# First loads in 256 KB pieces ordered by need, with a flight limit, and larger weight sums, in a two-layer convolution and joint kernel

## The chip, the cores and the metric

The kernel runs on one core of one Trainium2 chip. The time is the device time of one execution in microseconds (us), as a median of several executions. Engines are named as the profile names them: PE is TensorE's matmuls, PEld its weight loads, DVE is VectorE, ACT is ScalarE, POOL is GpSimd, SP is SyncE, which issues all loads here. All times inside an execution count from the start of its profiled span.

Ratios are the mean time of one kernel's fast runs over that of the other's fast runs of the same rounds, so they are not quite the ratios of the medians quoted beside them. The "granted clock" of a table is the share of PE's full clock that the chip allowed (1.00 is all of it).

## The reference, cut to what matters

```python
B, T, D, K, U = 2, 4000, 512, 5, 8            # x: [B,T,D], w1, w2: [K,D,D], all bf16
h = sum of 5 taps: xp[:, i:i+T, :] @ w1[i]    # then gelu, then every second row
f = sum of 5 taps: hp[:, i:i+T1, :] @ w2[i]   # then gelu, then every second row
fe = f @ w_f ; ge = g @ w_g
j = tanh(fe[:, :, None, :] + ge[:, None, :, :])
return j @ w_o                                 # [2, 1000, 8, 512]
```

Because only every second row of h is kept, the kernel works on four phases of the time axis (row number modulo 4). A fast-convolution scheme replaces part of the products: some operands are differences or sums of phases (named a0, a1, a2, a3, b1, b3), and some weights are sums of taps: 2·(tap 1 + tap 3), and (tap 0 + tap 4) minus or plus tap 2.

## The kernel before: the parts that matter

The first 1000 rows of layer 1 are split into two tiles, here "tile 1" (254 columns) and "tile 2" (246 columns); a larger "tile 3" follows. Tile 1's input comes by plain loads and is transposed on PE; all other inputs come by transposing DMA. In tile 1, output blocks m = 0 and 1 are computed directly from five taps, while blocks 2 and 3 use the operands and weight sums.

```python
for rt in range(2): load_xr(rt)                   # 2 x 512 KB of x
for i in (0, 1, 3, 4, 2): load_w1("sp", i)        # 5 taps x 512 KB
for ph in (2, 3, 1, 0): load_x(0, ph, 272, 528)   # tile 2, transposing DMA, then later tiles
...
warm_mm(12)                                       # matmuls on zeros while the loads travel
for pp in range(2):                               # pp 0: even phases, pp 1: odd phases
    for rt in range(2): ...                       # 8 PE transposes; pp 0 copied by DVE, pp 1 by ACT
...
for w in ("a0", "a1", "a2", "b3"): t0.xf(w)       # DVE operands of tile 1
for w in ("b1", "a3"): t0.shift(w); t0.xf(w)      # an ACT copy, then DVE
wsum13(...)                                       # DVE: add, then times 2
wsum04(..., 2); wsum04(..., 3)                    # DVE: 3 ops of 128x512 each
for i in (0, 1, 3): direct(i)                     # PE
filt("a0", "b1"); direct(4); filt("b3", "a3"); direct(2); filt("b2", "a1", "a2")
for w in ("a0", "b1", "a3"): t1.shift(w)          # tile 2, ACT
for w in ("a0", "b1", "b3", "a1"): t1.xf(w)       # tile 2, DVE
wsum04(..., 0); t1.xf("a2"); t1.xf("a3"); wsum04(..., 1)
... t0.gelu(0), t0.gelu(1), t0.post(2), t0.post(3)   # first evictions of tile 1 on DVE
```

Each engine runs its instructions in the order in which the program lists them. An instruction that waits holds up everything behind it on its engine: in the changed kernel below, DVE stands idle for 2.31 us until 11.66 us, although all inputs of a sum that is listed later had landed by 8.20 us.

## Time and profile before

| | |
|---|---|
| time, median of the 3 runs known at first | 281.95 us (281.63 to 282.59); with a fourth run 281.79 |
| PE busy, of a span of 280.3 us | 273.9 us |
| first weight matmul on PE | 8.99 us |
| DVE's first eviction of tile 1 starts | 26.12 us |
| chain of waits stays on PE from | 42.15 us |

The head of the page (span, then busy time of each engine, its share and its number of instructions), kernel before:

```profile
span 280.3 us, 3870 instructions
PE 273.9 (98%) x1436; PEld 137.8 (49%) x1436; DVE 188.0 (67%) x250; ACT 160.3 (57%) x191; POOL 30.2 (11%) x39
```

Averaged over the span, PE is the limit. The start is different. Next is the table by stage of the kernel before: per stretch its length, then the busy time of each engine, the granted clock, and the DMA share and rate. (The DMA share adds up packet times, and it can exceed 1.)

```profile
core 0: us, PE busy (x) PEld busy (x) DVE busy (x) ACT busy (x) POOL busy (x), PEclk, DMA share, GB/s
6.00:16.00 10.00, 8.95 (x98) 8.07 (x97) 8.68 (x13) 3.93 (x4) 0.18 (x3) 1.00 1.25 266
16.00:26.00 10.00, 10.00 (x96) 9.06 (x94) 9.42 (x16) 4.70 (x7) 0.12 (x1) 1.00 0.96 208
```

From 6 to 26 us DVE is busy for 18.1 of 20 us. It is nearly as full as PE (18.95 us). The list of waits of PE from 2 to 46 us (who waited for whom, total us, times, longest) shows how little PE waits:

```profile
PE acc L298 <- DMA w_sb<-in_w_dram: 1.1, 1, 1.1
PE acc L298 <- DVE xt_55 L287: 0.7, 2, 0.5
PE acc L298 <- DVE xs_50 L287: 0.2, 1, 0.2
```

The timeline of DVE (start, busy us, engine and line, operation, names, shapes, count) just before its first eviction, which is the last line (the first line is the sum of taps 1 and 3):

```profile
12.13 1.22 DVE L287 TENSOR_TENSOR w_t<-w_sb 128x2048 bf16<-128x2048 bf16 x1
13.38 0.69 DVE L423 TENSOR_SCALAR w_t<-w_t 128x2048 bf16<-128x2048 bf16 x1
...
21.10 0.68 DVE L287 TENSOR_TENSOR ssum_70<-w_sb 128x512 f32<-128x512 bf16 x1
21.82 1.29 DVE L287 TENSOR_TENSOR w_t<-ssum_70,w_sb 128x512 bf16<-128x512 f32 x2
23.03 0.67 DVE L287 TENSOR_TENSOR xs_49<-xs_49 128x984 bf16<-128x984 bf16 x1
23.61 0.67 DVE L287 TENSOR_TENSOR xt_54<-xt_54,xs_49 128x984 bf16<-128x984 bf16 x1
24.19 0.68 DVE L287 TENSOR_TENSOR ssum_71<-w_sb 128x512 f32<-128x512 bf16 x1
24.91 1.29 DVE L287 TENSOR_TENSOR w_t<-ssum_71,w_sb 128x512 bf16<-128x512 f32 x2
26.12 0.75 DVE L499 SCALAR_TENSOR_TENSOR ty_67<-acc,cs_65 128x254 f32<-128x254 f32 x2
```

From 21.10 us on, these lines follow one another with no idle time: weight sum of block 0, tile 2's operands a2 and a3, weight sum of block 1, first eviction. The chain of work that ended last (start, us, what) shows where DVE stops mattering:

```profile
40.89 1.12 DVE xt_55 L287
42.02 0.14 issue
42.15 234.13 PE acc L298 x1112
```

After 42.15 us PE runs almost to the end. So the time is what happens before that moment, plus a rest of about 240 us.

### The profile page before, as it was taken

To read this page: it belongs to the slowest core of one execution; us is meant where nothing else is said; L and a number is where in the kernel's file an instruction comes from. 1 tells how busy PE (TensorE), PEld (TensorE's weight loads), DVE (VectorE), ACT (ScalarE), POOL (GpSimd) and SP (SyncE) were. 2 spreads that over 40 slices of the span, in tenths; PEclk is the share of its full clock that TensorE was granted. 3 is DMA by queue.
4 is the path that set the end of the run, shared out by engine and by line. 5 is a ranking of instruction groups with operands and counts; after the bars stand their busy time and mean duration, and the time that the engine had idled before them with its cause. 6 is when DMAs were issued, how large, how long until landed. Compare 5 with 4: busy or idle time off the path is not lost.

```text
span 280.3 us, 3870 instructions
## 1 busy us (share of the span) xinstructions
PE 273.9 (98%) x1436; PEld 137.8 (49%) x1436; DVE 188.0 (67%) x250; ACT 160.3 (57%) x191; POOL 30.2 (11%) x39
## 2 busy tenths in 40 slices
PE   8899989999999999999999999999999999999995
PEld 3799934444444444444444444444444444444442
DVE  0989797956896766686424363676776775666764
ACT  2533949328426533932336565948957957966930
POOL 1000000099992000000000000000000000000000
PEclk9999999999999999999999999999999999999999
DMA  7999999990000000000000020444454445444444
GB/s 251 291 179 201 213 211 191 316 325 3 4 0 0 2 0 0 0 2 0 0 0 4 0 75 5 155 155 154 135 169 151 150 144 170 145 155 145 155 150 140
DMA packets 54719, 31.85 MB, mean 114 GB/s; under 512 B 31646, under 2 KB 54446, under 8 KB 54702
## 3 DMA queue, kind: packets, MB, share of 16 engines
q1 hardware_dynamic: 54702, 31.62, 41.8%
q8 instruction: 11, 0.18, 0.3%
q14 instruction: 6, 0.05, 0.1%
HBM read 7.86 MB, written 16.38 MB: 87 GB/s over the span
## 4 chain that ended last, share of the span: by engine, by line
PE 84%; SPq 6%; DVE 5%; issue 2%; ACT 1%; DMA 1%; DVEq 0%
PE acc L298 84%; SPq L330 4%; SPq L316 2%; DMA xs_49<-in_x_dram 1%; ACT xt_55 L291 1%; DVE xs_50 L287 1%; DVE xt_55 L287 1%; DVE w_t L287 1%; DVE ty_68 L499 1%; DVE ty_68 L287 0%; DVE xt_54 L287 0%; SPq L321 0%; DVE ty_67 L499 0%; DVE ty_69 L499 0%; DVE ssum_71 L287 0%
## 5 line engine op out<-in xcount | busy, mean ns | idle before, releaser
L298 PE MATMUL acc<-wo_sb,jT 128*128 128x512 bf16 (+1 forms) x504 | 108.3, 378 | 0.0
L298 PEld LDWEIGHTS acc<-wo_sb,jT 128*128 128x128 bf16 x504 | 49.3, 98 | 58.8
L298 PE MATMUL acc<-xt_55,w_sb 128*128 128x500 bf16 (+1 forms) x192 | 42.1, 357 | 0.2 <-DVE xt_55 L287 0.2
L291 ACT ACTIVATE jT<-feT_80,geT 128x1000 bf16<-128x1000 f32 (+6 forms) x44 | 35.8, 889 | 0.0
L291 ACT ACTIVATE jT<-feT_79,geT 128x1000 bf16<-128x1000 f32 (+4 forms) x40 | 35.1, 948 | 0.0
L298 PE MATMUL acc<-xt_54,w_sb 128*128 128x500 bf16 (+1 forms) x160 | 33.2, 342 | 0.0
L298 PEld LDWEIGHTS acc<-xt_55,w_sb 128*128 128x128 bf16 x192 | 18.6, 98 | 18.7 <-issue 0.9
L291 ACT ACTIVATE cs_65<-acc 128x500 f32<-128x500 f32 (+2 forms) x13 | 7.0, 538 | 27.3 <-PE acc L298 27.3
L298 PEld LDWEIGHTS acc<-xt_54,w_sb 128*128 128x128 bf16 x160 | 15.6, 98 | 13.0
L291 ACT ACTIVATE cs_66<-acc 128x500 f32<-128x500 f32 (+2 forms) x13 | 7.0, 536 | 21.8 <-PE acc L298 21.7
L298 PE MATMUL acc<-xs_49,w_sb 128*128 128x254 bf16 (+2 forms) x112 | 15.6, 286 | 1.1 <-DMA w_sb<-in_w_dram 1.1
L291 ACT ACTIVATE ost_93<-acc 128x512 bf16<-128x512 f32 x10 | 6.0, 597 | 16.4 <-PE acc L298 16.4
L679 DVE CAST ost_82<-acc 128x512 bf16<-128x512 f32 x11 | 7.6, 691 | 10.3 <-PE acc L298 10.3
L679 DVE CAST ost_88<-acc 128x512 bf16<-128x512 f32 x10 | 6.9, 692 | 10.3 <-PE acc L298 10.3
L298 PE MATMUL acc<-xs_49,w_t 128*128 128x246 bf16 (+2 forms) x72 | 13.8, 315 | 0.0
L287 DVE TENSOR_TENSOR ty_68<-ty_68,acc 128x1000 f32<-128x1000 f32 (+2 forms) x9 | 9.7, 1079 | 5.7 <-PE acc L298 5.7
L287 DVE TENSOR_TENSOR ty_67<-ty_67,acc 128x1000 f32<-128x1000 f32 (+2 forms) x9 | 9.7, 1078 | 5.1 <-PE acc L298 5.1
L298 PEld LDWEIGHTS acc<-xs_49,w_sb 128*128 128x128 bf16 x112 | 10.8, 97 | 4.0 <-DMA w_sb<-in_w_dram 1.2
L291 ACT ACTIVATE ost_87<-acc 128x512 bf16<-128x512 f32 x10 | 5.9, 593 | 11.4 <-PE acc L298 11.4
L287 DVE TENSOR_TENSOR ty_69<-ty_69,acc 128x1000 f32<-128x1000 f32 (+1 forms) x8 | 8.5, 1061 | 4.2 <-PE acc L298 4.1
L298 PE MATMUL acc<-xt_55,w_t 128*128 128x500 bf16 (+1 forms) x48 | 10.0, 341 | 0.5 <-DVE xt_55 L287 0.5
L679 DVE CAST ost_86<-acc 128x512 bf16<-128x512 f32 (+1 forms) x12 | 7.7, 646 | 2.6 <-PE acc L298 2.6
(116 smaller groups left out, 363.2 us busy)
## 6 DMA issues: line engine op xcount, KB each, us to landing
w_sb<-in_w_dram SPq DMA_DIRECT2D x10, 512.0 KB, 7.9
out_dram<-ost_82 SPq DMA_DIRECT2D x11, 128.0 KB, 1.9
out_dram<-ost_84 SPq DMA_DIRECT2D x10, 128.0 KB, 1.9
out_dram<-ost_86 SPq DMA_DIRECT2D x10, 128.0 KB, 1.9
out_dram<-ost_90 SPq DMA_DIRECT2D x10, 128.0 KB, 1.9
out_dram<-ost_83 SPq DMA_DIRECT2D x9, 128.0 KB
out_dram<-ost_85 SPq DMA_DIRECT2D x9, 128.0 KB
out_dram<-ost_87 SPq DMA_DIRECT2D x9, 128.0 KB
```

Of the source, the lines that this page charges most:

```text
L287: pl.op(eng, lambda e: e.tensor_tensor(out=o.ap, in0=a.ap, in1=b.ap, op=op), (a, b), (o,))
L291: pl.op("act", lambda e: e.activation(o.ap, i.ap, func, scale=scale, bias=0.0 if bias is None else bias.ap), rd, (o,))
L298: ins = e.matmul(o.ap, lhsT=l.ap, rhs=r.ap, start=start and n == 0, stop=stop and n == len(pairs) - 1, skip_group_check=not check)
L316: return pl.dma(eng, lambda e: e.dma_start(dst.ap, src), (), (dst,))
L330: pl.dma("sp", lambda e: e.dma_start_transpose(out=dst.ap, in_=src), (), (dst,))
L499: pl.op("dve", lambda e, o=o, f=f: e.scalar_tensor_tensor(out=o.ap, in0=d.ap, scalar=f, in1=c.ap, op0=ALU.mult, op1=add), (d, c), (o,))
L679: pl.op("dve", lambda e, o=o, v=v: e.tensor_copy(out=o.ap, in_=v.ap), (v,), (o,))
```

## The change

The intent is to start PE earlier. The first loads become pieces of 256 KB, in the order in which PE needs them, with at most four under way. PE then turns the even phases alone, starts with taps 0, 2 and 4 (which need only even phases), and turns the odd phases in between. The larger weight sums are meant to relieve DVE. The diff, cut:

```diff
-    NWARM = 12
+    NWARM = 7
+    FLIGHT = 4
...
+        def load_lead(dst, src):       # waits for the load issued FLIGHT places earlier
...
-            load_xr(rt)
-        for i in (0, 1, 3, 4, 2):
-            load_w1("sp", i)
+            load_xr(0, rt)                       # even phases, 256 KB each
+        for i in (0, 2, 4):
+            load_w1(i, 0)                        # output columns 0..255 of a tap
+        for rt in range(2):
+            load_xr(1, rt)                       # odd phases
+        for i, h in ((1, 0), (3, 0), (0, 1), (1, 1), (3, 1), (4, 1), (2, 1)):
+            load_w1(i, h)
...
-                if pp:
+                if rt:                           # of each pair of copies, one on DVE, one on ACT
                     act(o, pv, ACT.Copy)
...
+        turn(0)
+        warm_mm(3)
...
+            if eng == "dve":
+                act(v, v, ACT.Copy, scale=2.0)   # the doubling goes to ACT
-        def wsum04(wsb, wt, eng, m):
+        def wsum04(wsb, wt, eng, m, nm=1):       # nm blocks in one op
...
+        t0.shift("a0")
+        for w in ("a1", "a2", "a0"):
             t0.xf(w)
+        for i in (0, 2):
+            direct(i)
+        turn(1)
         for w in ("b1", "a3"):
             t0.shift(w)
+        for w in ("b3", "b1", "a3"):
             t0.xf(w)
+        for i in (4, 1, 3):
+            direct(i)
         wsum13(w1_sb, w1_t, "dve")
-        wsum04(w1_sb, w1_t, "dve", 2)
-        wsum04(w1_sb, w1_t, "dve", 3)
+        wsum04(w1_sb, w1_t, "dve", 2, 2)
+        filt("a0", "b1", "b3", "a3", "b2", "a1", "a2")
...                                               # both t0.gelu calls now come before t1.shift
-        for w in ("a0", "b1", "b3", "a1"):
+        for w in ("a0", "b1", "b3"):
             t1.xf(w)
-        wsum04(w1_sb, w1_t, "dve", 0)
-        t1.xf("a2")
-        t1.xf("a3")
-        wsum04(w1_sb, w1_t, "dve", 1)
+        wsum04(w1_sb, w1_t, "dve", 0, 2)
+        for w in ("a1", "a2", "a3"):
+            t1.xf(w)
```

More of the change, by code (lines that the diff above doesn't have):

```diff
@@ L264, in bass_standalone__seq2seq_rnn_t_joint__speech_kernel @@
         ty = [at(f"ty{i}", [2, NT], FP32) for i in range(3)]
-        ssum = [at(f"ssum{i}", [NK, P], FP32) for i in range(2)]
+        ssum = at("ssum", [NK, 2 * P], FP32)
         geT = at("geT", [NK * BU], FP32)
@@ L316, in load_w, with load_xr, load_w1 @@
             return pl.dma(eng, lambda e: e.dma_start(dst.ap, src), (), (dst,))
-        def load_xr(rt):
-            dst = xr[rt][:].map(lambda a: a.rearrange("p r k c -> p (r k c)"))
-            src = x[0, 4 * P * rt:4 * P * (rt + 1), :].rearrange("(p r) c -> p (r c)", r=4)
-            return pl.dma("sp", lambda e: e.dma_start(dst.ap, src), (), (dst,))
+        lead = []
+        def load_lead(dst, src):
+            o = pl.dma("sp", lambda e: e.dma_start(dst.ap, src), (), (dst,))
+            for d in lead[:max(0, len(lead) - FLIGHT + 1)][-1:]:
+                o.deps[("dma", d.idx)] = True
+            lead.append(o)
+        def load_xr(pp, rt):
+            src = x[0, 4 * P * rt:4 * P * (rt + 1), :].rearrange("(p r) c -> p r c", r=4)[:, pp::2, :]
+            dst = xr[rt][pp::2].map(lambda a: a.rearrange("p r k c -> p r (k c)"))
+            load_lead(dst, src)
+        def load_w1(i, h):
+            sl = slice(h * D // 2, (h + 1) * D // 2)
+            load_lead(w1_sb[i, :, sl], w1[i].rearrange("(k c) d -> c k d", c=P)[:, :, sl])
         def load_x(s, ph, lo, hi):
@@ L333, in bass_standalone__seq2seq_rnn_t_joint__speech_kernel @@
         for rt in range(2):
-            load_xr(rt)
-        def load_w1(eng, i):
-            load_w(eng, w1_sb[i], w1[i].rearrange("(k c) d -> c k d", c=P))
-        for i in (0, 1, 3, 4, 2):
-            load_w1("sp", i)
+            load_xr(0, rt)
[5 more added lines that the diff above has]
+            load_w1(i, h)
         for ph in (2, 3, 1, 0):
@@ L354, in bass_standalone__seq2seq_rnn_t_joint__speech_kernel, with turn @@
         psb = ps.h[:, :].bitcast(BF16)
-        for pp in range(2):
+        def turn(pp):
             for rt in range(2):
@@ L358, in bass_standalone__seq2seq_rnn_t_joint__speech_kernel, with fn @@
                 pv = View(psb[:, bk * 1024:(bk + 1) * 1024].rearrange("p (r k c) -> p r k c", r=2, k=NK), np.array([bk]), True)
-                def fn(e, rt=rt, pp=pp, pv=pv):
+                def fn(e, rt=rt, pv=pv):
                     for r in range(2):
@@ L364, in fn @@
                     return ins
-                pl.op("pe", fn, (xr[rt][:], ident[:]), (pv,))
+                pl.op("pe", fn, (xr[rt][pp::2], ident[:]), (pv,))
                 o = xs[0][pp::2, :, 16 + rt * P:16 + (rt + 1) * P]
-                if pp:
+                if rt:
                     act(o, pv, ACT.Copy)
@@ L383, in xf @@
             h = NT // 2
-            if which == "a0" and keep:
-                tt("dve", o(0), src[2, :, off - 1:off - 1 + n], ph(2), sub)
-            elif which == "b3" and keep:
+            if which == "b3" and keep:
                 tt("dve", dst[0, :, h:h + n], ph(3), ph(1), sub)
@@ L422, in wsum13 @@
             tt(eng, v, wsb[1, :, lo:hi], wsb[3, :, lo:hi], add)
-            pl.op(eng, lambda e: e.tensor_scalar(out=v.ap, in0=v.ap, scalar1=2.0, scalar2=None, op0=ALU.mult), (v,), (v,))
-        def wsum04(wsb, wt, eng, m):
-            sl = slice(m * P, (m + 1) * P)
-            s = ssum[m % 2][:]
+            if eng == "dve":
+                act(v, v, ACT.Copy, scale=2.0)
+            else:
+                pl.op(eng, lambda e: e.tensor_scalar(out=v.ap, in0=v.ap, scalar1=2.0, scalar2=None, op0=ALU.mult), (v,), (v,))
+        def wsum04(wsb, wt, eng, m, nm=1):
+            sl = slice(m * P, (m + nm) * P)
+            s = ssum[:, 0:nm * P]
             tt(eng, s, wsb[0, :, sl], wsb[4, :, sl], add)
@@ L531, in direct @@
                        [(w1_sb[i, k, m * P:(m + 1) * P], xs[0][r, k, 16 + d:16 + d + NA]) for k in range(NK)],
-                       i == 0 and s == 0, i == 2, False)
+                       i == 0 and s == 0, i == 3, False)
         base0 = {2: 4 * NT, 3: 6 * NT}
@@ L541, in filt @@
                     t0.product(w, m, o, w in ("a0", "b2"))
-        for w in ("a0", "a1", "a2", "b3"):
+        t0.shift("a0")
+        for w in ("a1", "a2", "a0"):
             t0.xf(w)
+        for i in (0, 2):
+            direct(i)
+        turn(1)
         for w in ("b1", "a3"):
             t0.shift(w)
+        for w in ("b3", "b1", "a3"):
             t0.xf(w)
+        for i in (4, 1, 3):
+            direct(i)
         wsum13(w1_sb, w1_t, "dve")
-        wsum04(w1_sb, w1_t, "dve", 2)
-        wsum04(w1_sb, w1_t, "dve", 3)
-        for i in (0, 1, 3):
-            direct(i)
-        filt("a0", "b1")
-        direct(4)
-        filt("b3", "a3")
-        direct(2)
-        filt("b2", "a1", "a2")
+        wsum04(w1_sb, w1_t, "dve", 2, 2)
+        filt("a0", "b1", "b3", "a3", "b2", "a1", "a2")
         for b in range(B):
@@ L561, in bass_standalone__seq2seq_rnn_t_joint__speech_kernel @@
             memset(hT[b][0, :, HOFF + NP2:HOFF + NP2 + 1])
+        for m in (0, 1):
+            t0.gelu(m, ps.pair(m * NT, 256, NA))
         for w in ("a0", "b1", "a3"):
             t1.shift(w)
-        for w in ("a0", "b1", "b3", "a1"):
+        for w in ("a0", "b1", "b3"):
             t1.xf(w)
-        wsum04(w1_sb, w1_t, "dve", 0)
-        t1.xf("a2")
-        t1.xf("a3")
-        wsum04(w1_sb, w1_t, "dve", 1)
-        for m in (0, 1):
-            t0.gelu(m, ps.pair(m * NT, 256, NA))
+        wsum04(w1_sb, w1_t, "dve", 0, 2)
+        for w in ("a1", "a2", "a3"):
+            t1.xf(w)
         for m, A in base0.items():
```

## The prediction

> **What bounds the kernel now.** The page gives TensorE (PE) 273.9 us busy of a 280.3 us span at full granted clock. Its gaps after the start are few: 1.05 us at 7.94 us (waiting for the first weights; list of waits) and 0.87 us at 39 to 42 us (waiting for VectorE, DVE). But the chain of waits is PE only after 42.15 us. Before that it runs through DMA issue, a transposed load landing at 20.49 us, then DVE and ScalarE (ACT) without slack: DVE is busy 18.3 of the 19.6 us from 6.6 to 26.2 us (stage table). So an early PE counts only if DVE is earlier too.
>
> **What the change removes.** Warm-up goes from 12 to 7+3 matmuls (0.43 us apart in the timeline): 0.85 us. The 1.05 us gap should go: the even-phase pieces allow transposes at about 4 us instead of 5.8, and real matmuls at 6.3 to 7.4 us instead of 8.99. First-tile PE work is unchanged (about 80 x 0.107 + 56 x 0.107 us), but the odd-phase transposes (1.0 us) now follow the start, so tile 2 could start on PE at 22 to 23 us instead of 23.65: about 1.2 us gained, at most 1.8.
> DVE sheds one 0.69 us scaling (ACT takes it, about 1.9 us by its 128x2000 copies of 1.86). Weight sums of 128x1024 instead of twice 128x512 (0.684 us each) save a fixed part: the Trainium skill ("VectorE: DVE Perf Modes", errata section) gives (N+151)/0.96 ns for an fp32 add, which agrees with 684 to 688 ns at N=512 here; estimate 1.22 us at 1024, so about 0.15 us per pair, 0.9 us in all.
>
> **What it adds.** Weight halves have 512 B runs. In the packet records 4096 B take 159 ns, 1024 B 46, 256 B 18; interpolated, 512 B take 27, so 2.6 MB of weights take an estimated 8.7 us instead of 7.4. The transposed loads, issued behind them, should land up to 1.7 us later (20.5 to 22 us for the fourth); DVE reaches their data later still, so this should not bind.
> The real cost is DVE waiting. Odd phases turn only after taps 0 and 2 (3.4 us of matmuls), at about 10 us; DVE waits for that and then for three ACT copies of 1.0 us. The weight sum follows at about 15 us instead of 12.1. ACT then owes scaling 1.9, two gelus 1.1 and the shifts, before DVE may start tile 2. Adding up: tile 2's last three operands, which now follow the whole second weight sum (3.4 us), are ready at 27 to 28.5 us; before, operands at 24.2 and sums at 26.1.
>
> **Critical path.** PE reaches tile 2 early, waits 2 to 4 us for those operands and finishes its first block 0.5 to 2 us later than before (26.6 us). The saturated ACT/DVE stretch to 42 us passes this on.
>
> **Prediction: 283.0 us**, range 280.8 to 284.8. Faster by over 2%: 0.02; within 2%: 0.95; slower by over 2%: 0.03.
>
> **What would show it.** Right: first weight matmul before 7.5 us; DVE idle over 3 us between 8 and 15 us; a new PE gap of 2 us or more between 22 and 28 us, released by DVE; the chain entering PE for good at 42.5 us or later. Wrong: no such gap, chain into PE before 41.5 us.
>
> **What would make it wrong.** If DVE is ready before 26 us, the early start survives and about 280.5 us follows. If the weights straggle (in before, three DMA engines ran up to 2 us behind the rest), the start slips towards 8 us and the time towards 285.

## The result, and the profile after

The changed kernel takes 284.63 us (284.55 to 285.02, 4 runs) against 281.79 us (280.92 to 282.59, 4 runs) for the kernel before. The ratio is 1.0104, 95% interval 1.0072 to 1.0136: slower by about 1%, which counts as the same at the 2% mark. The head of the page, kernel after:

```profile
span 282.5 us, 3883 instructions
PE 273.9 (97%) x1434; PEld 137.5 (49%) x1434; DVE 186.9 (66%) x243; ACT 163.0 (58%) x193; POOL 30.1 (11%) x39
```

PE's busy time is the same; DVE has 1.1 us less to do. The table by stage, kernel after:

```profile
6.00:16.00 10.00, 9.49 (x96) 8.15 (x94) 4.81 (x9) 5.09 (x5) 0.19 (x3) 1.00 0.95 270
16.00:26.00 10.00, 9.04 (x84) 7.95 (x82) 9.37 (x10) 6.27 (x8) 0.00 (x0) 1.00 1.08 183
```

In the first ten of these microseconds PE is busier than before (9.49 us against 8.95), but DVE does only 4.81 us of work where it did 8.68. What DVE waited for between 8 and 30 us, kernel after:

```profile
DVE xs_49 L387 <- PE acc L380: 2.3, 1, 2.3
DVE xt_55 L288 <- ACT xs_49 L292: 2.2, 2, 1.4
DVE xt_55 L288 <- ACT xt_55 L292: 0.7, 2, 0.4
DVE xt_54 L288 <- ACT xt_54 L292: 0.6, 2, 0.3
```

Of the second line, 1.43 us ended already at 7.48 us. The kernel before had 0.8 us of waits in the same stretch. The first wait can be found in the timeline of DVE, kernel after; the bracket gives the idle time just before and who ended it:

```profile
8.68 0.68 DVE L288 TENSOR_TENSOR xt_55<-xt_55,xs_49 128x1016 bf16<-128x1016 bf16 x1
11.66 0.69 DVE L387 COPY xs_49<-acc 128x1024 bf16<-128x1024 bf16 x1 [2.31 <-PE acc L380]
13.17 0.69 DVE L288 TENSOR_TENSOR xt_55<-xs_49 128x1016 bf16<-128x1016 bf16 x1 [0.81 <-ACT xs_49 L292]
...
15.79 1.22 DVE L288 TENSOR_TENSOR w_t<-w_sb 128x2048 bf16<-128x2048 bf16 x1
...
22.95 1.22 DVE L288 TENSOR_TENSOR ssum<-w_sb 128x1024 f32<-128x1024 bf16 x1
24.20 2.36 DVE L288 TENSOR_TENSOR w_t<-ssum,w_sb 128x1024 bf16<-128x1024 f32 x2
26.48 0.67 DVE L288 TENSOR_TENSOR xt_54<-xs_49 128x984 bf16<-128x984 bf16 x1
...
28.35 0.74 DVE L520 SCALAR_TENSOR_TENSOR ty_67<-acc,cs_65 128x254 f32<-128x254 f32 x2
```

After its third operand DVE idles until PE has transposed the odd phases, at 11.66 us. The sum of the tap weights starts at 15.79 us (before: 12.13 us). Tile 2's a1 comes at 26.48 us, behind the whole weight sum of blocks 0 and 1, and the first eviction at 28.35 us, 2.23 us later than before. PE's waits from 2 to 46 us, kernel after:

```profile
PE acc L299 <- DVE xt_54 L288: 2.2, 1, 2.2
PE acc L299 <- DVE xt_55 L288: 0.7, 2, 0.5
PE acc L299 <- issue: 0.5, 1, 0.5
PE acc L380 <- DMA xr_64<-in_x_dram: 0.4, 1, 0.4
PE acc L299 <- DVE xs_50 L288: 0.2, 1, 0.2
```

The first line is new: PE waits 2.2 us for tile 2's a1. The waits at 42 to 44 us (0.7 and 0.2 us) are as long as before. The chain, kernel after:

```profile
44.23 0.14 issue
44.37 234.13 PE acc L299 x1112
```

The chain settles on PE 2.22 us later, and the rest has the same length, 234.13 us, as before. So the first weight matmul came 1.45 us earlier (7.54 us instead of 8.99). PE's first matmul of tile 2 came only 0.57 us earlier (23.19 us instead of 23.76), because 0.9 us of transposes now lie behind the start; and inside tile 2's first block the early start was lost and about 2.2 us on top.

### The profile page after: what moved, and what is told of

Its sections match the earlier page's. It is cut to its first block, busy times and chain, and to the rows that moved or that the text cites. A ratio compares the mean times of both kernels' runs of the same rounds, so it can differ in the third digit from the quotient of the medians.

```text
span 282.5 us, 3883 instructions
## 1 busy us (share of the span) xinstructions
PE 273.9 (97%) x1434; PEld 137.5 (49%) x1434; DVE 186.9 (66%) x243; ACT 163.0 (58%) x193; POOL 30.1 (11%) x39
## 4 chain that ended last, share of the span: by engine, by line
PE 85%; DVE 6%; ACT 4%; issue 2%; DMA 2%; SPq 0%; DVEq 0%
PE acc L299 84%; ACT xt_55 L292 2%; DMA xr_64<-in_x_dram 2%; DVE w_t L288 1%; DVE xs_50 L288 1%; DVE xt_55 L288 1%; ACT w_t L292 1%; ACT xt_54 L292 1%; ACT hT_61 L292 1%; PE acc L380 1%; DVE ty_68 L520 1%; DVE xt_54 L288 0%; DVE ty_68 L288 0%; DVE ssum L288 0%; ACT xs_49 L292 0%
```

## The experiments

Theory A: the kernel is bound, up to about 42 us, by DVE's queue together with ACT's. The changed order leaves DVE idle early and then puts the weight sum of blocks 0 and 1 and tile 2's operands late in the queue. Theory B: the load scheme (smaller runs, the flight limit, later transposed loads) makes everything late.

All results in one table; the kernel before ran beside each group on the same chip. The first eviction on DVE, and the end of the last PE gap before PE runs through, are read from each kernel's timeline and chain of waits. All ratios are against the kernel before.

| kernel | first weight matmul, us | DVE's first eviction, us | last PE gap ends, us | median, us | ratio (95% interval) |
|---|---|---|---|---|---|
| before | 8.99 | 26.12 | 42.15 | 281.79 | |
| after | 7.54 | 28.35 | 44.37 | 284.63 | 1.0104 (1.0072 to 1.0136) |
| e1_fill | 8.01 | 25.69 | 41.72 | 281.65 | 1.0018 (0.9997 to 1.0038) |
| e2_nolimit | 7.42 | 28.22 | 44.23 | 284.60 | 1.0122 (1.0106 to 1.0139) |
| e3_oldloads | 7.89 | 28.69 | 44.71 | 284.64 | 1.0136 (1.0107 to 1.0164) |
| e4_bigsums | 8.68 | 24.53 | 40.54 | 280.57 | 0.9992 (0.9962 to 1.0022) |
| e5_pool | 7.30 | 26.04 | 42.05 | 282.31 | 1.0034 (1.0018 to 1.0050) |
| e6_start | 8.24 | 25.10 | 41.11 | 280.89 | 0.9978 (0.9961 to 0.9995) |
| e7_startpool | 8.55 | 25.86 | 41.87 | 282.07 | 1.0019 (1.0004 to 1.0034) |
| e8_oddearly | 8.34 | 28.77 | 44.79 | 284.89 | 1.0117 (1.0101 to 1.0134) |
| e9_split | 7.57 | 29.06 | 45.10 | 285.26 | 1.0134 (1.0107 to 1.0161) |
| e10_sumfirst | 7.99 | 23.80 | 39.81 | 280.09 | 0.9951 (0.9926 to 0.9975) |
| e11_halftap | 7.15 | 23.26 | 39.29 | 279.63 | 0.9930 (0.9907 to 0.9953) |
| e12_oddfill | 8.48 | 25.87 | 41.89 | 282.19 | 1.0016 (0.9993 to 1.0040) |

The kernel before had medians of 281.14 us beside e1 to e4, 281.56 us beside e5 to e8 and 281.57 us beside e9 to e12.

Two things can be read from the columns. The last gap ends 16.01 to 16.04 us after the first eviction in all fourteen kernels, and the median is 239.6 to 240.4 us more than that. The column of the first weight matmul does not order the times: the changed kernel starts at 7.54 us and takes 284.63 us, e6_start begins at 8.24 us and takes 280.89 us.

Two limits of this reading. In e4_bigsums and e10_sumfirst the last gap is only 0.09 and 0.05 us long. There PE runs through from its first weight matmul (the chain of e10_sumfirst), so that PE's work since its start and DVE's queue end together, and an earlier DVE alone would gain nothing more:

```profile
7.99 31.77 PE acc L298 x272
39.76 0.05 issue
39.81 20.40 PE acc L298 x96
```

And part of the scatter in the first column does not come from the edits. In these traces PE works at half its pace at first: up to a certain moment its transposes start one per 0.107 us, after it one per 0.056 us. The moment differs from execution to execution: 5.10 us in e11_halftap, 5.38 in the changed kernel, 6.38 in e10_sumfirst, 6.70 in e1_fill. It falls on the first entry of the trace's record of PE's clock; the granted clock in the tables by stage does not show it. e1_fill has the loads and PE order of the changed kernel and yet starts 0.47 us later.

What the granted clock does show later in the run is no rival cause. Two of the four runs of the changed kernel had a mean granted clock of 0.994 and took 284.56 and 284.71 us; the two at 0.999 and 1.000 took 284.55 and 285.02 us.

### e1_fill: the weight sum into DVE's idle stretch

```diff
         for w in ("a1", "a2", "a0"):
             t0.xf(w)
+        wsum04(w1_sb, w1_t, "dve", 0, 2)
         for i in (0, 2):
             direct(i)
...
-        wsum04(w1_sb, w1_t, "dve", 0, 2)
         for w in ("a1", "a2", "a3"):
```

> Edit: the changed kernel with one thing moved: the weight sum of the first two output blocks, which needs only pieces landed by 8.2 us, goes on VectorE to its idle stretch after the first three tile-1 operands (9.4 to 11.7 us). Loads, TensorE order and ScalarE order stay. Theory A (VectorE idles early and then owes the sum in front of tile 2's operands): the PE gap of 2.16 us at 25 us falls under 0.6 us, the chain enters PE for good about 1.5 to 2.2 us earlier than the 44.4 us of the changed kernel, time 282.4 to 283.1. Theory B (late loads, by small pieces and the flight limit, set the stretch): no or little change, 284.3 to 284.8.

The median is 281.65 us, 3.0 us under that of the changed kernel (by the ratios, which were taken beside the kernel before each time, 1.0018 instead of 1.0104, so about 2.4 us); that is a little more than expected. PE's gap before tile 2 vanished. The timeline of DVE, e1_fill:

```profile
9.74 1.22 DVE L288 TENSOR_TENSOR ssum<-w_sb 128x1024 f32<-128x1024 bf16 x1
10.99 2.36 DVE L288 TENSOR_TENSOR w_t<-ssum,w_sb 128x1024 bf16<-128x1024 f32 x2
13.27 0.68 DVE L387 COPY xs<-acc 128x1024 bf16<-128x1024 bf16 x1
...
25.69 0.74 DVE L520 SCALAR_TENSOR_TENSOR ty<-acc,cs 128x254 f32<-128x254 f32 x2
```

The three operations of the sum run where DVE had stood idle, and the first eviction moves from 28.35 to 25.69 us. Loads, PE's order and ACT's order are those of the changed kernel, and the fourth transposed load of tile 2 landed no earlier (23.63 us, 23.38 in the changed kernel). Theory B cannot explain this. But the result only equals the kernel before; the early PE start still gives nothing.

### e2_nolimit and e3_oldloads: undo the load scheme

```diff
-    FLIGHT = 4
+    FLIGHT = 14                                  # e2_nolimit
```

```diff
-   fourteen pieces, at most four under way
+   for rt in range(2): load_xr(rt)              # e3_oldloads: 2 x 512 KB
+   for i in (0, 2, 4, 1, 3): load_w("sp", w1_sb[i], ...)   # 5 x 512 KB, no limit
```

> Edit: the changed kernel with the flight limit of 4 raised to 14, so no load waits for an earlier one. Theory A: loads and the tile-2 transposed loads land 1 to 2 us earlier, but the order of VectorE and ScalarE work stays; time 283.8 to 284.8, and the PE gap before tile 2's a1 stays over 1.5 us. Theory B: the limit cost the time; 282.0 to 283.0.

> Edit: the changed kernel with the loads of before: two whole 512 KB blocks of the input, then five whole 512 KB taps in order 0, 2, 4, 1, 3, no limit. All compute order stays as changed. Theory A: first weight matmul back at about 9 us, second transposes at about 12.5 us instead of 11.0, so VectorE is later still; 284.8 to 286.5, slower than the changed kernel. Theory B: the loads were the fault, so 282.5 or less.

By the DMA completion records, the fourth transposed load of tile 2 lands at 23.38 us in the changed kernel, at 21.27 us without the limit and at 19.77 us with the old loads. The time did not move: 284.60 and 284.64 us. DVE meets the same waits in both: 2.3 us for the odd phases' transposes and then 0.81 us for an ACT copy. So the load scheme alone is not what costs the time, nor is it what the changed order gains from. In e3_oldloads tap 0 landed at 7.79 us, so PE started at 7.89 us, earlier than the 9 us that I had expected; hence the time lies just under the expected range.

### e4_bigsums: the other part of the change alone

```diff
 # on the kernel before
+            if eng == "dve": act(v, v, ACT.Copy, scale=2.0)
-        wsum04(w1_sb, w1_t, "dve", 2)
-        wsum04(w1_sb, w1_t, "dve", 3)
+        wsum04(w1_sb, w1_t, "dve", 2, 2)
...
-        wsum04(w1_sb, w1_t, "dve", 0)
+        wsum04(w1_sb, w1_t, "dve", 0, 2)
         t1.xf("a2")
         t1.xf("a3")
-        wsum04(w1_sb, w1_t, "dve", 1)
```

> Edit: the kernel before with the other part of the change alone: weight sums in 128x1024 operations, the doubling of the tap 1+3 sum on ScalarE. Theory A: VectorE sheds 1.5 us before 26 us, but the fourth transposed load at 20.5 us holds part of it; VectorE starts the first eviction 0.3 to 0.9 us earlier, time 281.0 to 281.6 (before 281.8). Theory B says nothing of it: the same time as before. If the larger sums themselves were the fault, it would be slower than before by over 0.5 us.

The first eviction comes 1.6 us earlier, more than expected, and PE's waits from 38 to 42 us shrink to 0.09 us. The median is 280.57 us (expected were 281.0 to 281.6) beside 281.14 us, but one of the four runs took 281.75 us, and the interval of the ratio includes 1. The larger sums, with the doubling on ACT, were not at fault; by the profile they help, by the measured times this is not certain. ACT's part in the changed kernel was not tested alone: with its new order, DVE waits for ACT's copies for tile 2 twice, 0.32 and 0.24 us.

### e5_pool and e7_startpool: the sum on GpSimd

```diff
 # e5_pool on the changed kernel; e7_startpool the same on e6_start
+        for m in (0, 1):
+            wsum04(w1_sb, w1_t, "pool", m)       # with a scratch of its own
...
-        wsum04(w1_sb, w1_t, "dve", 0, 2)
```

> Edit: the changed kernel, with the same weight sum of the first two output blocks taken off VectorE altogether and done on GpSimd, which is idle there (six operations of 128x512, 1.2 to 2.0 us each by its later ones, so done by about 24 us). Theory A (VectorE is what is late): the PE gap at 25 us goes, and now the fourth transposed load at about 23.4 us holds VectorE; first eviction on VectorE at about 25 us instead of 28.4, time 281.0 to 282.0. If the stretch were set by the loads in the changed kernel, no change: 284.3 to 284.8.

> Edit: e6_start with the weight sum of the first two output blocks on GpSimd instead of VectorE, which frees 3.4 us of VectorE before its first eviction. If PE is bound by its start alone, equal to e6_start within 0.3 us; if VectorE still binds in e6_start, up to 0.8 us less: 279.2 to 280.2.

e5_pool recovered most (282.31 us) and missed its range by 0.3 us. e7_startpool missed by more: at 282.07 us it is 1.2 us slower than e6_start. The reason is in DVE's timeline, e5_pool:

```profile
14.00 3.10 DVE L290 TENSOR_TENSOR xt<-xt,xs 128x1016 bf16<-128x1016 bf16 x2
```

Two operations of 0.69 us each took 3.10 us together. In those microseconds POOL ran this (timeline of POOL, e5_pool):

```profile
13.52 3.04 POOL L290 TENSOR_TENSOR w_t<-psum__71,w_sb 128x512 bf16<-128x512 f32 x2
```

The Trainium skill ("SBUF — State Buffer", section "SBUF: two separate sides") says that DVE and GpSimd share a port pair under an exclusive lock, which also holds for a DVE operation with two SBUF inputs against a GpSimd operation that reads SBUF, and that the other fully blocks. The trace fits this: 0.69 us became 1.55 us per operation, and in e7_startpool POOL's own first operation took 2.19 us where it took 1.15 to 1.41 us in e5_pool. No run here tested the lock apart from this mix. Handing work to an idle GpSimd gave back part of DVE's gain in e5_pool, and more than all of it in e7_startpool: there DVE shed 3.6 us of sums, and the operations beside POOL's took about 5 us more than in e6_start.

### e6_start: fewer warm-ups on e4_bigsums

```diff
-    NWARM = 12
+    NWARM = 9
```

> Edit: the kernel before with large sums and ScalarE doubling (e4_bigsums) and 9 warm-up matmuls instead of 12. In e4_bigsums PE had no gap over 0.1 us after its start at 8.7 us, so there the start itself should count. Theory A: the first weight matmul comes at 7.6 to 8.6 us, the time is 0.3 to 1.0 us under e4_bigsums, 279.6 to 280.3. If VectorE still binds, the gaps at 39 to 42 us come back and the time stays at 280.5.

PE started 0.45 us earlier than in e4_bigsums, yet the time was no better (280.89 us beside a before of 281.56 us). The waits for DVE at 38 to 41 us came back, 0.75 us in all. In that execution the first transposed load landed at 16.33 us (14.10 us in e4_bigsums), and DVE waited for ACT's copy of it. This is the other branch of the expectation: DVE still bound.

### e8_oddearly and e12_oddfill: take away the wait for the odd phases

```diff
 # e8_oddearly on the changed kernel
-        load order: even phases, taps 0 2 4, odd phases, ...
+        load order: even phases, odd phases, taps 0 2 4, ...
         turn(0)
-        warm_mm(3)
+        turn(1)
...                                               # b1, a3, b3 of tile 1 right after a1, a2, a0
 # e12_oddfill: e8_oddearly, and
+        wsum04(w1_sb, w1_t, "dve", 0, 2)         # right after those operands
...
-        wsum04(w1_sb, w1_t, "dve", 0, 2)         # no longer in front of tile 2's a1
```

> Edit: the changed kernel with its odd phases loaded right after the even ones and turned right after them, before taps 0 and 2, and the three extra warm-ups dropped; piece sizes, limit, sums and the order on VectorE of everything later stay. Theory A (waiting for the late odd phases is what VectorE loses): VectorE idles under 2 us between 8 and 16 us, first eviction on it at 26.0 to 27.0 us instead of 28.4, time 282.3 to 283.3 although the first weight matmul comes later (8.5 to 9.5 us). If only the place of the sum in the order counts, the gap of 2 us and 284.5 stay.

> Edit: e8_oddearly (changed kernel, odd phases early) with the sum of output blocks 0 and 1 moved into the 3.5 us in which VectorE waited there for taps 1 and 3. If that new wait is why e8_oddearly gained nothing: first eviction on VectorE at 25.2 to 25.8 us instead of 28.8, no PE gap of 2 us at 25 us, time 281.4 to 282.2. If something else holds tile 2, it stays over 284.

e8_oddearly contradicted Theory A as I had put it: 284.89 us. (Its profile shows a granted clock of 0.81 from 26 to 35 us; DVE's operations take as long there as in the other profiles.) The wait for the odd phases did go, but another took its place. The timeline of DVE, e8_oddearly:

```profile
16.21 1.23 DVE L288 TENSOR_TENSOR w_t<-w_sb 128x2048 bf16<-128x2048 bf16 x1 [3.47 <-DMA w_sb<-in_w_dram]
```

The sum of taps 1 and 3 needs all four of their halves, and the last of them landed at 16.08 us. The pieces had been ordered by PE's need; DVE needs the halves of taps 1 and 3 sooner than PE does. In the changed kernel DVE's operands of the odd phases (done at 15.79 us) and these halves (the last at 15.19 us) come at nearly the same time. So neither undoing the loads (e2, e3) nor undoing the late odd phases (e8) helped alone. e12_oddfill confirms it: with the available sum put into that wait, the first eviction comes at 25.87 us instead of 28.77 (expected were 25.2 to 25.8) and the time is 282.19 us.

### e9_split: give PE its operands earlier, leave DVE's work

```diff
-        wsum04(w1_sb, w1_t, "dve", 0, 2)
+        wsum04(w1_sb, w1_t, "dve", 0)
         for w in ("a1", "a2", "a3"):
             t1.xf(w)
+        wsum04(w1_sb, w1_t, "dve", 1)
```

> Edit: the changed kernel with the weight sum of output blocks 0 and 1 split in two again, as before: block 0, then tile 2's last three operands, then block 1. So PE gets its operands about 1.5 us earlier, while VectorE has slightly more work (three fixed parts of about 0.15 us) before its first eviction. If VectorE's whole queue binds, as Theory A has it: the PE gap at 25 us falls to under 1.2 us, and yet the time does not fall: 284.4 to 285.2, chain into PE at 44.4 to 45.0 us. If the PE gap itself is the cost: about 1 us less, 283.2 to 283.9.

PE's gap before a1 shrank from 2.16 to 0.92 us, as expected, and the time did not fall: 285.26 us, a little above the expected range, while the intervals of the ratios of e9_split and of the changed kernel overlap. PE waited 0.83 us for block 1's weights instead and 0.68 us at tile 3, and the first eviction moved to 29.06 us. The visible gap was a symptom; the length of DVE's queue up to the first eviction was the cost.

### e10_sumfirst and e11_halftap: a version that beats both

```diff
 # e10_sumfirst on e6_start
         wsum04(w1_sb, w1_t, "dve", 2, 2)
+        wsum04(w1_sb, w1_t, "dve", 0, 2)
...
-        wsum04(w1_sb, w1_t, "dve", 0, 2)         # was between a1 and a2 of tile 2
 # e11_halftap: e10_sumfirst, and tap 0 alone in two halves, the needed half first
```

> Edit: e6_start (kernel before, large sums, ScalarE doubling, 9 warm-ups) with the sum of output blocks 0 and 1 moved in front of tile 2's operands, into about 1.5 us in which VectorE waited there for transposed loads. Expected: first eviction on VectorE 0.8 to 1.1 us earlier than the 25.1 us of e6_start, no PE gap over 0.2 us at 38 to 42 us, time 0.4 to 0.9 us under e6_start: 279.9 to 280.4 against a before of 281.5.

> Edit: e10_sumfirst with tap 0 alone loaded in two halves, the half that PE needs first in front. In e6_start the first weight matmul waited 0.5 us for tap 0 (landed at 8.19 us). Expected: that half lands about 0.7 us earlier, the wait goes, time up to 0.5 us under e10_sumfirst, 279.5 to 280.2; if the slowest DMA engines set it, no difference beyond 0.2 us.

Both times lie in the expected ranges. In e10_sumfirst DVE has work while the transposed loads travel: the first eviction comes at 23.80 us, 1.3 us earlier than in e6_start, which is more than expected. In e11_halftap the needed half of tap 0 landed at 6.63 us (tap 0 in e10_sumfirst: 7.94 us), and PE's waits from 2 to 46 us come down to one line, e11_halftap:

```profile
PE acc L298 <- DVE xt L287: 0.2, 1, 0.2
```

With 279.63 us, ratio 0.9930 (0.9907 to 0.9953), e11_halftap is faster than the kernel before by 0.7% and than the changed kernel by about 5 us. It is still within 2% of before. The intervals of e10 and e11 overlap, so what the half tap alone is worth (0.46 us by the medians) is not settled. Nor do the profiles settle it: in e10_sumfirst PE waited 0.31 us for tap 0, but its last transpose also started at 7.45 us instead of 6.84 us, because the change of PE's pace, told above, came 1.28 us later.

## Why the prediction was right or wrong

The prediction said 283.0 us with 280.8 to 284.8; the time is 284.63 us. The direction and the mechanism held, and the range held by 0.17 us; the size was too small.

- "An early PE counts only if DVE is earlier too": right. In fourteen kernels the time follows DVE's first eviction and not PE's start. The branch "If DVE is ready before 26 us, the early start survives and about 280.5 us follows" did not come true: e1_fill had its first eviction at 25.69 us and took 281.65 us.
- "DVE idle over 3 us between 8 and 15 us": right, 2.31 + 0.81 + 0.40 = 3.5 us.
- "A new PE gap of 2 us or more between 22 and 28 us, released by DVE": right, 2.16 us. "The chain entering PE for good at 42.5 us or later": right, 44.37 us.
- "First weight matmul before 7.5 us": just missed, 7.54 us. The second even-phase piece landed at 5.72 us and PE waited 0.45 us for it.
- The mis-sized step is "finishes its first block 0.5 to 2 us later than before"; 283.0 us is only about 1 us above the kernel before. From the timelines of PE the block ended about 2.3 us later (its last product started at 28.58 us; before, at 26.29 us). The start was some 0.7 us later than the middle of my 6.3 to 7.4 us, so the odd phases turned at 11.0 us, not at "about 10", and the sum of taps started at 15.79 us, not at "about 15". The last operand was ready at 28.43 us, at the late end of "27 to 28.5", and tile 2 started on PE at 23.19 us, not at "22 to 23". Then "the saturated stretch passes this on" held to the full: 2.23 us at the first eviction became 2.22 us at the end of the chain. The measured difference of the medians is 2.84 us; between the two profiles it is 2.2 us of span, and the rest is within the spread of the kernel before (280.92 to 282.59 us).
- "The real cost is DVE waiting" was right, but naming the odd phases as its cause was incomplete. e8_oddearly took that wait away and the wait for taps 1 and 3 replaced it at once.
- The estimate of 1.22 us for a sum of 128x1024, from the formula of the Trainium skill ("VectorE: DVE Perf Modes", section on the errata), was right: 1.219 and 1.222 us on average by the groups of DVE instructions.
- The estimate of 27 ns for a 512 B packet was right: the median in the packet records is 27 ns. The transposed loads came later than expected (the fourth by 2.9 us, not 1.7), and as predicted it did not bind: ACT waited 1.66 us for it, but DVE used it only at 26.48 us, and e2_nolimit and e3_oldloads gained nothing by getting it earlier.

## What to carry to other kernels

Before you start the busiest engine earlier, find out which engine's queue sets the end of the opening stage. Here it was DVE's, and putting already available work into its idle time was worth 2.4 to 3 us, while starting PE 1.45 us earlier was worth nothing as long as DVE's queue ended later. When you order loads by need, count the needs of every engine: a weight that PE needs last may be an operand that the vector engine needs first. When taking a wait away changes nothing, look for the next wait in the same queue before you drop the theory.

## What the Trainium skill lacked or had wrong

- "DMA: Bandwidth & Descriptors" (Specifications) gives 512 B as the least transfer for line rate. Here the median packet took 27 ns at 512 B, 46 ns at 1024 B and 159 ns at 4096 B. Size over time on 16 engines gives 303, 356 and 412 GB/s, so 512 B is well under the rate of 4096 B. What arrived shows the same: 290 GB/s from 10 to 14 us in e2_nolimit (512 B, no flight limit; median packet 31 ns) against 393 GB/s from 3 to 4.5 us in the kernel before (4096 B). The section "Why small descriptors are slow (HBM only)" explains the direction with a fixed cost per packet, but gives no such times.
- No page that I read gives by how many us the 16 engines of one load spread, or how this varies. In the kernel before, tap 0 was done on 13 engines by 6.91 us and on the last at 8.95 us. With the same loads of the kernel before up to tap 0, its landing lay at 7.17 us (e4), 7.79 us (e3), 7.94 us (e10), 8.19 us (e6) and 8.51 us (e7).
- No page that I read gives the cost of going from copies to transposing loads on one queue. In the kernel before, the first packets of the first transposing load took up to 2.3 us instead of 18 ns, and ended at 14.54 to 14.58 us, just before the last copy's completions arrived (14.63 to 14.81 us). What makes them wait was not tested.
- "SBUF — State Buffer" (SBUF: two separate sides) states the exclusive port lock, which fits what was seen; it lacks what the lock costs in such a mix: 0.69 us became 1.55 us for a 128x1016 bf16 operation beside GpSimd's 128x512 one (e5_pool).
